# A thresholded attention with a two-layer MLP behind it: the first six periods and the order of the score products are rebuilt

## The chip, the cores and the metric

The kernel runs on one core of a Trainium2 chip. The core has a matrix engine (TensorE, PE in the profile, its weight loads PEld), VectorE (DVE), ScalarE (ACT), GpSimd (POOL), and a synchronisation engine (SyncE, SP) that issues most of the transfers. Each engine takes its own instructions strictly in the order in which the program gives them; engines wait for one another by semaphores. The metric is the device time of one execution in microseconds (us).

## What is computed

Eight batches of eight heads, 576 positions, head dimension 64. Scores are scaled products of q and k; each row keeps only the scores within tau = 0.02 of its maximum, and a softmax over what is left weighs v. The heads are put side by side, 4608 tokens of 512 numbers, and go through two matrix products with a leaky rectifier between them.

```python
scores = scale * np.matmul(q, k.transpose(0, 1, 3, 2))
thresh = np.max(scores, axis=-1, keepdims=True) - tau
scores = np.where(scores >= thresh, scores, -1000000000.0)
scores = scores - np.max(scores, axis=-1, keepdims=True)
attn = np.exp(scores)
attn = attn / (np.sum(attn, axis=-1, keepdims=True) + 1e-09)
x = np.matmul(attn, v)          # heads side by side: [4608, 512]
h = x @ w_in                    # [512, 2048]
out = np.maximum(0.01 * h, h) @ w_out
```

## The kernel before

**Splitting and turning.** q and k arrive as fp32 with positions on the partitions. A *unit* is one pair of heads of q or of k in one batch, or the 64-position tail of all pairs ("t"); a batch has ten units. Each is multiplied by 64 and split into a high fp16 part and a low one, so that three fp16 products (high-high, low-high, high-low) stand for one exact product. On GpSimd the split is `split_scale`, `split_high`, `split_low` (L144, L150, L154); `split_now` (L164, L165) does it on ScalarE and VectorE. TensorE then transposes the two parts into a PSUM tile `tp` (L183), and a copy, usually ScalarE's (L186, L190), puts them into `qT` or `kT`. The k tail is copied once more on GpSimd (L188).

**Periods.** 72 periods, nine for a batch: two blocks of 256 queries for each of the four head pairs, and one period for the tails. In a period the score products (L227, 24 of them, three for each of eight pieces) fill one PSUM tile `sc` of five banks: four places of 576 columns, two query halves c by two heads h. The two heads sit in the two row halves of TensorE. Two pieces of different heads share a bank; a signal, an empty GpSimd instruction (L246), keeps the later one behind the earlier. VectorE copies each place to SBUF and takes its minimum on the way (`copies`, L257; the sign is turned), makes the thresholds `th` (L259), and for three of the four places multiplies the exps by the mask (`weights`, L282). ScalarE makes the exps (L271), and for the fourth place the masked exps by itself (`exp_steep`, L276 and L277). The reciprocal of the sums (`rec`, L288) is spread over a strip of the weights by GpSimd (`widen`, L292), and one transposing DMA on SyncE (`turn_w`, L297) makes `wT`.

**Two periods later** PV multiplies v by `wT` (L309) and VectorE evacuates the product, scaled by the reciprocals (L321, L329), into a token group. Groups are queued for layer 1 (L349, with the leaky rectifier on ScalarE, L351) and layer 2 (L362, evacuated at L368): at most two calls of layer 1 and four of layer 2 in each period, and what is left over runs behind the last period. `tp`, `pv` and `hp` (layer 1's products) share two PSUM buffers, which go round in the order of the program.

**The order of the work** is written out by hand. The main loop gives each period's instructions; four tables (`loads_at`, `turns_at`, `pool_at`, `low_at`) say which loads, transposes and splits go into which period. In one period the loop gives, in this order: scores, the four copies, the widening and transposing DMA of the period before, low splits, loads, stores, transposes with their copies, GpSimd's other work, the exps with layers 1 and 2 between them, PV, the weights with the evacuation between the second and third, the reciprocal. Ahead of the loop the first loads are issued (pair 0 and 1 on SyncE's and ScalarE's queues, the k tail on SyncE's, the four parts of `w_in` on GpSimd's, right at the start), and the units pair 0 k, pair 0 q and k tail are split and turned:

```python
first = units(0)
for key in first[:3]:
    split_now(key)
turn(first[0])
turn(first[1], nc.vector.tensor_copy)
turn(first[2])
```

In what follows, the functions that the change touches are given with the line numbers of the profile.

## Time and profile before

| what | us |
|---|---|
| median of 3 runs (lowest, highest) | 527.41 (526.46, 530.69) |
| profiled execution: own time, span of its instructions | 526.85, 525.1 |
| busy: PE, VectorE, ScalarE, GpSimd | 472.8, 435.1, 422.3, 256.3 |
| first score copy (L257) starts | 16.04 |
| first layer-1 product (L349); last attention period's first copy | 63.78; 483.3 |
| scores of one period: 24 products at 26.0, at 83.5 | 3.10, 1.64 |
| transposing DMA, median from issue to landing | 5.9 |

The span runs from the first instruction to the last. Busy time is the time in which an engine executes; the time in which it waits is listed with the instruction that ended the wait. For this kernel the first 90 us differ from the rest: after them the periods nearly repeat every nine. A line of the timeline gives the start, the duration, the engine, the line, the operation, the tiles written and read, the number of instructions merged into the line, and in brackets the idle time before it and who ended it. SPq stands for SyncE's queue, where the duration is that of issuing.

### The profile page before, as it was taken

What the parts mean: (1) busy time and instruction counts of PE and PEld (TensorE: products, weight loads), DVE (VectorE), ACT (ScalarE), POOL (GpSimd) and SP (SyncE); (2) the same over time, 40 slices, a digit from 0 to 9 for tenths busy, and PEclk for the clock granted to TensorE, in tenths of its full rate; (3) what the DMA queues carried; (4) which work ended last, traced back from release to release, by engine and by line L of the source; (5) the groups of instructions that cost most, each with busy time, mean ns of one, the idle gap of its engine ahead of it and who ended that gap; (6) DMA issues with size and microseconds to landing.
All of it is one profiled execution on the core that took longest, in us unless ns stands there. A gap on an engine that the chain in (4) does not pass through costs nothing. (4 is left out here: it accounts for less than half of the span.)

```text
span 525.1 us, 18850 instructions
## 1 busy us (share of the span) xinstructions
PE 472.8 (90%) x7744; PEld 372.1 (71%) x7744; DVE 435.1 (83%) x1231; ACT 422.3 (80%) x714; POOL 256.3 (49%) x410
## 2 busy tenths in 40 slices
PE   4666768998989999999999999999999999999995
...
DVE  1778868999899999999899989999899989999300
...
GB/s 204 241 178 175 201 199 209 112 171 195 205 179 183 123 225 227 173 146 203 215 171 176 170 207 215 160 130 225 201 155 202 158 192 144 122 102 151 133 42 61
DMA packets 230806, 90.34 MB, mean 172 GB/s; under 512 B 201024, under 2 KB 227648, under 8 KB 230720
## 3 DMA queue, kind: packets, MB, share of 16 engines
...
## 5 line engine op out<-in xcount | busy, mean ns | idle before, releaser
L257 DVE TENSOR_SCALAR_CACHE_REDUCE s<-sc 128x576 f32<-128x576 f32 x288 | 199.0, 748 | 12.0 <-PE sc L227 11.5
L282 DVE SCALAR_TENSOR_TENSOR w<-s,th,e 128x576 f16<-128x576 f32 x216 | 184.2, 876 | 8.6 <-ACT e L271 1.1
L271 ACT ACTIVATE e<-s,mn 128x576 f16<-128x576 f32 x216 | 158.7, 773 | 20.2 <-DVE s L257 19.2
L362 PE MATMUL o<-wout,g 128*64 128x512 f16 x1152 | 148.9, 380 | 5.0 <-ACT osb L368 3.5
L349 PEld LDWEIGHTS <-win 128*64 128x64 f16 x2560 | 127.4, 110 | 29.2 <-issue 16.0
L349 PE MATMUL hp<-x,win 128*64 128x256 f16 x2048 | 134.4, 273 | 8.4 <-ACT kT L190 4.5
L227 PE MATMUL sc<-kT,qT 64*128 64x256 f16 (+7 forms) x1920 | 128.4, 298 | 12.0 <-DVE s L257 4.7
L292 POOL CAST w<-rec 128x256 f16<-128x256 f32 x72 | 28.7, 399 | 211.8 <-DVE rec L288 199.6
L227 PEld LDWEIGHTS <-qT 64*128 64x128 f16 (+1 forms) x1920 | 97.9, 101 | 35.0 <-issue 19.5
L351 ACT ACTIVATE g<-hp 128x512 f16<-128x512 f32 x144 | 84.6, 588 | 13.0 <-PE hp L349 13.0
L362 PEld LDWEIGHTS <-g 128*64 128x64 f16 x1152 | 69.6, 110 | 35.5 <-issue 8.5
L154 POOL TENSOR_TENSOR half<-scaled,half 128x512 f16<-128x512 f32 (+1 forms) x77 | 82.5, 1079 | 0.6
L309 PE MATMUL pv<-wT,v 128*64 128x256 f16 (+1 forms) x960 | 55.6, 251 | 12.2 <-DMA wT<-w 6.7
L309 PEld LDWEIGHTS <-v 128*64 128x64 f16 x960 | 44.6, 112 | 25.9 <-POOL v L105 5.3
L277 ACT ACTIVATE w<-s,minus_tau 128x576 f16<-128x576 f32 x72 | 55.8, 775 | 5.8
L276 ACT ACTIVATE s<-s,th 128x576 f32<-128x576 f32 x72 | 55.8, 775 | 0.9 <-DVE th L259 0.9
L183 PE MATMUL tp<-ident,half 128*64 128x128 f16 x1152 | 49.3, 236 | 8.0 <-ACT half L164 5.1
L150 POOL CAST half<-scaled 128x512 f16<-128x512 f32 (+1 forms) x77 | 52.1, 676 | 4.9
L183 PEld LDWEIGHTS <-half 128*64 128x64 f16 x1152 | 38.6, 119 | 22.1 <-issue 15.9
L190 ACT COPY kT<-tp 128x1024 f16<-128x1024 f16 x32 | 32.3, 1010 | 21.4 <-PE tp L183 21.4
L144 POOL TENSOR_SCALAR scaled<-raw 128x512 f32<-128x512 f32 x62 | 40.7, 657 | 10.2 <-DMA raw<-in_q_dram 8.3
L190 ACT COPY qT<-tp 128x1024 f16<-128x1024 f16 x31 | 31.4, 1014 | 14.1 <-PE tp L183 14.0
...
## 6 DMA issues: line engine op xcount, KB each, us to landing
...
win<-in_moe_w_in_dram POOLq DMA_DIRECT2D x4, 512.0 KB, 11.5
...
wT<-w SPq DMA_TRANSPOSE x72, 5.9
...
```

The source lines that it names most:

```text
L154: nc.gpsimd.tensor_tensor(out=halves[key][:, 1, 0:n, :, :], in0=scaled.pop(key)[:, 0:n, :, :], in1=halves[key][:, 0, 0:n, :, :], op=AX.sub ...
L183: nc.tensor.transpose(o, half[:, x, t, h, :], ident[:, :])
L190: copy(out=dst[:, :, p, ds(c0, 512)], in_=tp[:, :, :, :].rearrange("d x t p -> d x (t p)"))
L227: yield nc.tensor.matmul(out=o, lhsT=lhs, rhs=turned[st.b, "k"][rows, kx, pair, ds(key0, n)], start=(i == 0), stop=(i == 2), skip_group_ch ...
L257: nc.vector.tensor_scalar(out=st.s[t][:, :], in0=sc[:, ds(PLACE[t], 576)], scalar1=-1.0 / UNIT, scalar2=None, op0=AX.mult, op1=AX.min, acc ...
L271: nc.scalar.activation(out=st.e[t][:, :], in_=st.s[t][:, :], func=AF.Exp, bias=st.mn[:, n : n + 1], scale=-1.0)
L276: nc.scalar.activation(out=z, in_=z, func=AF.Prelu, bias=st.th[:, n : n + 1], scale=-1.0, alpha=1e20)
L282: nc.vector.scalar_tensor_tensor(out=w_of(st, t), in0=st.s[t][:, :], scalar=st.th[:, n : n + 1], in1=st.e[t][:, :], op0=AX.is_le, op1=AX.mult,
L309: nc.tensor.matmul(out=o, lhsT=v16[st.b % 2][:, 2 * c + u if st.tail else st.p, blk, :], rhs=rhs, start=(i == 0), stop=(i == 4), skip_grou ...
L349: nc.tensor.matmul(out=hp[ds(64 * c, 64), jj, :], lhsT=w_in16[:, i, ds(128 * j + 64 * c, 64)], rhs=g.x[:, i, :], start=(i == 0), stop=(i = ...
L351: nc.scalar.activation(out=g.g[:, ds(nj * u, nj), :], in_=hp[:, :, :], func=AF.Prelu, bias=0.0, scale=1.0, alpha=0.01)
L362: nc.tensor.matmul(out=g.o[ds(64 * c, 64), :], lhsT=g.g[:, j, ds(128 * m + 64 * c, 64)], rhs=w_out16[:, j, :], start=(j == 0), stop=(j == ...
```

## The change

The order and the place of work change; the amount of arithmetic doesn't.

- **Start.** The k tail is loaded first, on GpSimd's queue. The units are split, turned and copied one after another: k tail, pair 0 k, pair 0 q; the tail's and q's copies are VectorE's, k's is ScalarE's. Pair 1 is split by ScalarE and VectorE (`split_now`) where GpSimd did it; GpSimd splits pair 2 ahead of the loop and pair 3 in period 0, each one period sooner than before. `w_in`'s four loads move from the start into periods 1 and 2, `w_out`'s from periods 3 to 6 into 4 to 7. The v casts move one period ahead, the tail's first. The q tail's split and turn move from periods 2 and 3 to 6 and 7.
- **Batch 1's units** are turned in periods 3, 4, 5, 6, 6, 7, 8, 8, 9, 10 instead of two in each of 4 to 8; their scale and high part come two periods before, the low part one. Two of its loads come a period later.
- **Scores.** The order of the pieces changes, and the signal between the pieces that share a bank comes early, after the three products of a piece of place (1,1) instead of (1,0); in periods 0 to 3 it is an empty instruction of ScalarE. The first copy (place (0,0)) is given as soon as its own two pieces and the next one are out, and later products are declared free of it.
- **Every period.** The reciprocal of a period moves behind the second copy of the next one. The low splits come ahead of the widening. `turn` only transposes; `take` copies. Both transposes of a period are given first, then one copy, the first exp, the other copy.
- **Periods 2 to 5.** PV and its evacuation come ahead of layers 1 and 2 and of the weights, and a finished group is ready in the same period.

```diff
-    def load_tails(b, which):
+    def load_tails(b, which, eng=None):
         t = sb.tile([128, 2, 2, 64], FP32, tag="rawt", bufs=2, name="rawt")
         src = SRC[which][b, :, MAIN:S, :].rearrange("(u sh) p d -> u p sh d", u=2)
         for u in range(2):
-            nc.sync.dma_start(out=t[ds(64 * u, 64), :, :, :].rearrange("p s h d -> p (s h) d"), in_=src[u])
+            (eng or nc.sync).dma_start(out=t[ds(64 * u, 64), :, :, :].rearrange("p s h d -> p (s h) d"), in_=src[u])
...
-    def turn(key, copy=None):
-        copy = copy or nc.scalar.copy
+    def turn(key):
         b, p, which = key
-        dst, half = turned_of(b, which), halves.pop(key)
+        half = halves.pop(key)
         n = 2 if p == "t" else 4
-        c0 = 0 if which == "q" else 64
         if p == "t":
-            c0 = MAIN if which == "q" else 0
             tp = ps.tile([128, 2, 2, 2, 64], FP16, tag="h", bufs=2, name="tp")
         else:
             tp = ps.tile([128, 2, 4, 128], FP16, tag="h", bufs=2, name="tp")
...
                 for h in range(2):
                     o = tp[ds(64 * h, 64), x, :, t, :] if p == "t" else tp[ds(64 * h, 64), x, t, :]
                     nc.tensor.transpose(o, half[:, x, t, h, :], ident[:, :])
+        tps[key] = tp
+
+    def take(key, copy=None):
+        copy = copy or nc.scalar.copy
+        b, p, which = key
+        dst, tp = turned_of(b, which), tps.pop(key)
         if p == "t":
+            c0 = MAIN if which == "q" else 0
             for x in range(2):
                 copy(out=dst[:, x, :, ds(c0, 64)], in_=tp[:, x, :, :, :].rearrange("d u s p -> d (u s) p"))
             if which == "k":
                 nc.gpsimd.tensor_copy(out=dst[:, :, :, 576:640], in_=dst[:, :, :, 0:64])
         else:
+            c0 = 0 if which == "q" else 64
             copy(out=dst[:, :, p, ds(c0, 512)], in_=tp[:, :, :, :].rearrange("d x t p -> d x (t p)"))
...
+    TILES = ((0, 0), (0, 1), (1, 0), (1, 1))
+
     def scores(st):
 
+        st.mn = sb.tile([128, 4], FP32, tag="mn", bufs=2, name="mn")
+        st.th = sb.tile([128, 4], FP32, tag="th", bufs=2, name="th")
+        st.s, st.e = {}, {}
         (a00, a01), (b01, b00) = pieces(0, 0), pieces(0, 1)
         (a11, a12), (b12, b11) = pieces(1, 0), pieces(1, 1)
-        todo = [[(1, a12), (0, a00), (0, a01), (1, a11)], [(0, b00), (0, b01), (1, b11), (1, b12)]]
+        todo = [[(0, a00), (0, a01), (1, a11), (1, a12)], [(1, b12), (1, b11), (0, b01), (0, b00)]]
         todo = [[(c, x, i) for c, x in row for i in range(3)] for row in todo]
-        at_, signal = [0, 0], None
+        at_, signal, first = [0, 0], None, None
         while todo[0] or todo[1]:
             h = 1 if not todo[0] or (todo[1] and at_[1] < at_[0]) else 0
             c, x, i = todo[h].pop(0)
             at_[h] += x[1]
             for mm in product(st, c, h, x, i):
-                if (h, x) == (1, b12) and i == 0:
+                if first is not None:
+                    tc.declare_no_dep(mm.ins, first.ins, reason="other banks")
+                if (h, x) == (0, a12) and i == 0:
                     tc.add_manual_dep(mm.ins, signal.ins.name, BEHIND, reason="the row halves share a bank")
                 last = mm
-            if (h, x) == (0, a12) and i == 2:
-                signal = nc.gpsimd.nop()
+            if (h, x) == (1, b12) and i == 2:
+                signal = (nc.scalar if st.n < 4 else nc.gpsimd).nop()
                 tc.add_manual_dep(signal.ins, last.ins.name, BEHIND, reason="the row halves share a bank")
-
-    TILES = ((0, 1), (0, 0), (1, 0), (1, 1))
-
-    def copies(st):
-        st.mn = sb.tile([128, 4], FP32, tag="mn", bufs=2, name="mn")
-        st.th = sb.tile([128, 4], FP32, tag="th", bufs=2, name="th")
-        st.s = {}
-        for n, t in enumerate(TILES):
-            st.s[t] = sb.tile([128, 576], FP32, tag=f"s{n}", bufs=1, name="s")
-            nc.vector.tensor_scalar(out=st.s[t][:, :], in0=sc[:, ds(PLACE[t], 576)], scalar1=-1.0 / UNIT, scalar2=None,
-                                    op0=AX.mult, op1=AX.min, accum_out=st.mn[:, n : n + 1])
+            if (h, x) == (0, a11) and i == 2:
+                first = copy_min(st, 0)
+
+    def copy_min(st, n):
+        st.s[TILES[n]] = sb.tile([128, 576], FP32, tag=f"s{n}", bufs=1, name="s")
+        return nc.vector.tensor_scalar(
+            out=st.s[TILES[n]][:, :], in0=sc[:, ds(PLACE[TILES[n]], 576)], scalar1=-1.0 / UNIT, scalar2=None,
+            op0=AX.mult, op1=AX.min, accum_out=st.mn[:, n : n + 1])
+
+    def copies(st, before):
+        copy_min(st, 1)
+        if before:
+            recip(before)
+        copy_min(st, 2)
+        copy_min(st, 3)
         nc.vector.tensor_scalar(out=st.th[:, :], in0=st.mn[:, :], scalar1=1.0, scalar2=tau_f, op0=AX.mult, op1=AX.add)
         st.w = sb.tile([128, 2, 10, 128], FP16, tag="w", bufs=3, name="w")
         st.sum = sb.tile([128, 2, 2], FP32, tag="sum", bufs=3, name="sum")
-        st.e = {}
...
-    def finish(st):
+    def recip(st):
...
-    def evacuate(st, n):
+    def evacuate(st, ready):
...
-            l1q.extend((xg, u, nu, n + 1) for u in range(nu))
+            l1q.extend((xg, u, nu, ready) for u in range(nu))
...
     def split_at(n, key):
-        if key[0]:
-            at(pool_at, n - 2, lambda key=key: split_scale(key))
-            at(pool_at, n - 2, lambda key=key: split_high(key))
-            at(low_at, n - 1, lambda key=key: split_low(key))
-        else:
-            at(pool_at, n - 1, lambda key=key: split_pool(key))
-        at(turns_at, n, lambda key=key: turn(key))
+        at(pool_at, n - 2, lambda key=key: split_scale(key))
+        at(pool_at, n - 2, lambda key=key: split_high(key))
+        at(low_at, n - 1, lambda key=key: split_low(key))
+        at(turns_at, n, key)
 
     for b in range(1, B):
         base = PERB * (b - 1)
         for i, (s, w_) in enumerate(((0, "k"), (0, "q"), (1, "k"), (1, "q"))):
-            at(loads_at, base + ((-2, -1, 2, 3)[i] if b > 1 else (1, 1, 3, 3)[i]),
+            at(loads_at, base + ((-2, -1, 2, 3)[i] if b > 1 else (1, 1, 3, 4)[i]),
                lambda b=b, s=s, w_=w_: load_main(b, s, w_))
         for i, w_ in enumerate("kq"):
-            at(loads_at, base + ((-1, 5)[i] if b > 1 else (2, 4)[i]), lambda b=b, w_=w_: load_tails(b, w_))
+            at(loads_at, base + ((-1, 5)[i] if b > 1 else (2, 5)[i]), lambda b=b, w_=w_: load_tails(b, w_))
         for i, key in enumerate(units(b)):
-            split_at(base + 2 + 8 * i // 10 if b > 1 else base + 4 + i // 2, key)
+            split_at(base + 2 + 8 * i // 10 if b > 1 else (3, 4, 5, 6, 6, 7, 8, 8, 9, 10)[i], key)
     for b in range(B):
         base = PERB * (b - 1)
         if b:
             for s in range(2):
                 at(loads_at, base + 5 + s, lambda b=b, s=s: load_v(b, s))
             at(loads_at, base + 6, lambda b=b: load_vtails(b))
-        for p in range(NP):
-            at(pool_at, base + 8 + p if b else 2 + p // 2, lambda b=b, p=p: cast_v(b, p))
-        at(pool_at, base + 8 if b else 2, lambda b=b: cast_vtails(b))
-
-
+            for p in range(NP):
+                at(pool_at, base + 8 + p, lambda b=b, p=p: cast_v(b, p))
+            at(pool_at, base + 8, lambda b=b: cast_vtails(b))
+
+
+    load_tails(0, "k", nc.gpsimd)
     masks.make_identity(nc, ident[:, :])
     nc.gpsimd.memset(minus_tau[:, :], -tau_f)
     load_pair(0, "k", nc.sync)
     load_pair(0, "q", nc.scalar)
-    load_tails(0, "k")
+    load_pair(1, "k", nc.sync)
     load_pair(1, "q", nc.scalar)
-    load_pair(1, "k", nc.sync)
     for p in (2, 3):
         load_pair(p, "k", nc.sync)
         load_pair(p, "q", nc.sync)
...
     for t in v16:
         nc.gpsimd.memset(t[64:128, :, 4, :], 0.0)
         nc.gpsimd.memset(t[0:64, :, 5, :], 0.0)
+
+    first = units(0)
+    for key in (first[2], first[0], first[1]):
+        split_now(key)
+        turn(key)
+        take(key, None if key == first[0] else nc.vector.tensor_copy)
+    for key in first[3:5]:
+        split_now(key)
+    for key in first[5:7]:
+        split_pool(key)
+    for i, key in enumerate(first[3:9]):
+        at(turns_at, i // 2, key)
+    for key in first[7:9]:
+        at(pool_at, 0, lambda key=key: split_pool(key))
+    at(pool_at, 6, lambda: split_pool(first[9]))
+    at(turns_at, 7, first[9])
     for i in range(4):
-        load_w(i)
-        at(pool_at, 3 + i, lambda i=i: load_w(4 + i))
-
-    first = units(0)
-    for key in first[:3]:
-        split_now(key)
-    turn(first[0])
-    turn(first[1], nc.vector.tensor_copy)
-    turn(first[2])
-    for i, key in enumerate(first[3:]):
-        if i < 2:
-            split_pool(key)
-            at(turns_at, 0, lambda key=key: turn(key))
-        else:
-            split_at((0, 0, 1, 1, 2, 2, 3)[i], key)
+        at(pool_at, 1 + i // 2, lambda i=i: load_w(i))
+        at(pool_at, 4 + i, lambda i=i: load_w(4 + i))
+    at(pool_at, 1, lambda: cast_vtails(0))
+    for p in range(NP):
+        at(pool_at, 1 + p // 2, lambda p=p: cast_v(0, p))
+
+    def pv_of(n, ready):
+        if n >= PV_LAG and n - PV_LAG < N:
+            pv(periods[n - PV_LAG])
+            return lambda: evacuate(periods[n - PV_LAG], ready)
+        return lambda: None
 
     N = len(periods)
     n = 0
     while n < N + PV_LAG or l1q or l2q or stores:
         st = periods[n] if n < N else None
+        before = periods[n - 1] if 1 <= n <= N else None
+        early = n < 6
         if st:
             scores(st)
-            copies(st)
-        if 1 <= n <= N:
-            widen(periods[n - 1])
-            turn_w(periods[n - 1])
+            copies(st, before)
+        elif before:
+            recip(before)
         for f in low_at.get(n, []):
             f()
+        if before:
+            widen(before)
+            turn_w(before)
         for f in loads_at.get(n, []):
             f()
         while stores:
             store()
-        for f in turns_at.get(n, []):
-            f()
+        keys = turns_at.get(n, [])
+        for key in keys:
+            turn(key)
+        for key in keys[:1]:
+            take(key)
+        if st:
+            exp_plain(st, 0)
+        for key in keys[1:]:
+            take(key)
         for f in pool_at.get(n, []):
             f()
-        if st:
-            exp_plain(st, 0)
+        if early:
+            pv_of(n, n)()
         for half in range(2):
             if l1q and l1q[0][3] <= n:
                 layer1()
...
                     exp_plain(st, 2)
                 else:
                     exp_steep(st, 3)
-        if n >= PV_LAG and n - PV_LAG < N:
-            pv(periods[n - PV_LAG])
+        x = (lambda: None) if early else pv_of(n, n + 1)
         if st:
             weights(st, 0)
             weights(st, 1)
-        if n >= PV_LAG and n - PV_LAG < N:
-            evacuate(periods[n - PV_LAG], n)
+        x()
         if st:
             weights(st, 2)
-            finish(st)
         n += 1
```

2 lines of the change are left out of this document (1 added, 1 removed).

## The prediction

> **What bounds it now.** I read the page's busy shares first, then its 40 slices.
>
> ```profile
> PE 472.8 (90%) x7744; PEld 372.1 (71%) x7744; DVE 435.1 (83%) x1231; ACT 422.3 (80%) x714; POOL 256.3 (49%) x410
> ...
> PE   4666768998989999999999999999999999999995
> DVE  1778868999899999999899989999899989999300
> ```
>
> The slices are 13 us long. PE is full from the eighth on and has holes only before. The windows view puts a number on the middle:
>
> ```profile
> 86.40:435.00 348.60, 335.02 (x5735) 265.77 (x5732) 323.33 (x919) 311.35 (x526) 188.30 (x300) 1.00 0.87 180
> ```
>
> From period 9 to 62 PE (first pair of numbers) idles 13.6 us in 349, VectorE (third) 25. PE executes in order and its work is fixed, so the end moves only by PE idle time that goes or comes. It idles 33 us before 100 us (5.1 ahead of its first instruction, the rest gaps), 13.5 between 100 and 480. The waits up to 100 us name the holes (total, times, longest):
>
> ```profile
> DVE s L257 <- PE sc L227: 11.5, 4, 7.8
> PE pv L309 <- DMA wT<-w: 6.2, 2, 3.4
> PE pv L309 <- POOL v L105: 4.8, 2, 4.3
> PE sc L227 <- POOLq L246: 3.5, 3, 2.3
> ```
>
> I mark time by c(n), the first score copy (L257) of period n on the timeline: 16.0, 23.0, 30.6, 41.1, 47.7, 54.3, 61.9, 69.4, 79.4, 86.4 for n = 0 to 9. The 54 periods from there to 435.1 last 6.46 on average, so periods 2 (10.5) and 7 (10.0) are the bad ones. The lines behind them:
>
> ```profile
> 15.18 0.82 PE L227 MATMUL sc<-kT,qT 64*128 64x256 f16 x5 [2.31 <-POOLq L246]
> ...
> 16.04 0.76 DVE L257 TENSOR_SCALAR_CACHE_REDUCE s<-sc 128x576 f32<-128x576 f32 x1 [7.81 <-PE sc L227]
> ...
> 24.03 3.14 SPq L297 DMA_TRANSPOSE wT<-w  x1
> ...
> 27.22 0.57 SPq L72 DMA_DIRECT2D raw<-in_k_dram  x1
> ...
> 31.51 0.62 POOL L144 TENSOR_SCALAR scaled<-raw 128x512 f32<-128x512 f32 x1 [0.35 <-DMA raw<-in_k_dram]
> ...
> 34.30 2.49 POOL L105 CAST v<-vraw 128x256 f16<-128x256 f32 x4
> ...
> 62.65 8.74 SPq L297 DMA_TRANSPOSE wT<-w  x1
> ...
> 75.51 0.83 PE L309 MATMUL pv<-wT,v 128*64 128x256 f16 x10 [3.36 <-DMA wT<-w]
> ```
>
> The first copy waits for all 24 products, and these for a signal queued on POOL behind splits. In period 2 POOL waits for batch 1's k, which SP could issue only behind the transpose of period 0; the v casts come after that and PV of period 0 ends at 38.1. In period 7 a transpose shares the DMA with weight loads and lands 12.8 after its issue.
>
> **The start.** k tails go first, on POOL's queue. No row has them there. Bounds: 2.5 from issue to landing (SP's quickest tail load, at 34.99) and 8.2 (POOL's first weight load, at 2.70). I take 5.0 as the landing time, near SP's load, because the tails are small and nothing is ahead of them. The Trainium skill, page "DMA: Bandwidth & Descriptors", section "Anatomy of one DMA — SWDGE (gpsimd) path", gives about 2.0 us plus size. By that estimate the tails are there before pair 0's k (4.6) and all of the start is 0.4 earlier. No row here shows it alone.
> Then the tail, k and q go one after another, where before they overlapped. ScalarE: tail 5.0-5.5, k 5.6-6.2 (0.33 a piece). VectorE: tail and its copies to 6.7, k to 7.4. PE turns k by 8.0; ScalarE copies it (0.99) to 9.1 and only then splits q, to 9.8; VectorE to 10.2, PE 10.9, copy (0.68) 11.65. Scores start at 11.75, against 10.38 before: 1.4 lost. Behind that signal stand the period's transposed copies and exps, which need PE's transposes, and those come after the products anyway; so it holds up nothing. The two tail issues delay POOL's identity by 1.2 to 1.7 (its weight issues took 0.6 to 0.84), hidden until the first transpose at 5.6. Cold, 19 products take 2.5 and 24 take 3.1 (rows at 10.38 and 25.98). The signal now follows the split of pair 1 on ScalarE, done by 11.1, so the 2.3 stall goes; the first copy waits for 19 of 24. c(0) = 14.3, 1.8 earlier, with 13.3 to 16 as ends.
>
> **Periods 0 and 1.** PE turns pair 1 behind the scores, to 16.8. ScalarE: k copy, one exp, q copy, two exps, steep pair, to 21.9. Its signal for period 1 is queued behind all that, so the last products run 21.9 to 22.5; c(1) = 21.5, and the second copy waits for 22.5. The reciprocal now stands behind that copy: 23.3. It was 22.7. Widening 23.6, transpose issued 24.0: as before. c(2) comes out at 29.1 the same way (row 30.6).
>
> **POOL in periods 1 to 3 is the step that decides.** Its list for period 1 begins with the split of batch 1's k, whose load is still issued on SP behind that transpose: 24.0 + 3.1, landing 4.2 later (row at 27.22), 31.4. Behind the waiting instruction are queued two weight loads, the v tail casts, the casts of pairs 0 and 1, the low split, and then the widening of period 1, which was ahead of this wait before. By rows: scale and high 1.3, two loads 1.2, tails 0.85, pair 0 1.25: 36.2, PV of period 0 ends 36.9 (was 38.1). In the first six periods its evacuation stands ahead of the weights on VectorE, so these follow at 37.4 and end about 40.2: c(3) = 40.3, 0.8 gained. Pair 1 1.25, low 1.15: widening 38.6, transpose 39.1. It was 31.2. It lands 7.4 later (4.9 unloaded, 12.8 the longest; the nearest beside a weight load was 9.2 and 7.0, and four weight loads now fall in 33 to 50): 46.5. PV of period 1 can't run before, PE and VectorE stand, then 0.9 + 0.4 + three weights at 0.8: c(4) = 50.3, 2.6 late, from 48 to 53. Period 2 in the same way (widening 45.6, landing 53.5): c(5) = 57.2, 2.9 late. From period 3 POOL's list is short and the wait is gone; two layer-1 units now run in period 5. c(6) +2.5, c(7) +1.6. In period 7 the 3.4 wait can recur, since the w_out loads come a period later, beside v: I take half, so c(8) and c(9) come out even with before. **Early: 0, ends -4 and +5.**
> The weight loads are issued in busy periods: four in the quiet start took 2.37, 0.59 each, and w_out beside work 0.82 to 0.84, so 1.0 more, in the ends. The Trainium skill speaks against it: "SBUF — State Buffer", section "SBUF: two separate sides", says that POOL cannot write descriptors while VectorE holds the port pair they share. By that each issue would wait out a VectorE instruction (0.75 to 1.15), 3 to 4.6 for the four, and c(5) would be that much later still; the 0.82 rows say a quarter of it.
>
> **Periods 9 to 13.** Layer 1 of the first token group moves from periods 6-9 to 5-8. The next group is ready at period 10 in both, so the end's backlog stays; period 9 loses two units and 12 to 13 four layer-2 calls. PE would save 3.5, but VectorE alone needs about 5.8 a period: 0.8 gained.
>
> **The steady periods.**
>
> ```profile
> DVE rec L288 <- ACT w L277: 10.7, 23, 0.9
> ...
> PE hp L349 <- ACT kT L190: 6.2, 10, 0.7
> ...
> PE o L362 <- ACT osb L368: 2.8, 8, 0.6
> ...
> PE pv L309 <- DMA wT<-w: 0.5, 1, 0.5
> ```
>
> The reciprocal no longer waits for ScalarE's sum ahead of the first copy; VectorE gains 0.2 to 0.5 a period. PE gains only what it idled for VectorE's sake: the osb waits, unnamed gaps ahead of layer 2 (1.5), waits for evacuations and copies (2.4). That is 6.7; I take 4.5. The 6.2 of hp waits stay, as PE waits there for the first transposed copy in both. In exchange the reciprocal is 1.5 later, and so are widening, transpose and landing. PV starts about 3.45 after c and has waited once; late by 1.5, the transposes of periods 14, 15, 33, 51, 59 and 60 (latencies with queueing of 8 to 9.3) make it wait 0.1 to 1.5 each: 3.0 lost. The second transposed copy behind the first exp frees its PSUM buffer about when layer 1 needs it (0.68 + 0.9 against 1.75): 0.5 lost. **Steady: -1.0.** With nothing new it would be -4.5, with no gain +3.5.
>
> **Sum.** 526.85 (span 525.1 and 1.7 around it) + 0 - 0.8 - 1.0 = 525.0. The median 527.41 is 0.6 above that execution, inside its runs' 526.46 to 530.69, so I keep 525.
>
> **Rivals.** *POOL's order costs nothing that wasn't lost anyway* (27%): the start's 1.8 stays, period 7's 3.4 does not return, the 0.8 and the steady 4.5 come without new waits: 526.85 - 10.5 = 516.4. For it: the weight loads leave the start, and PE idles 28 in gaps before 100. Against: widening of period 1 behind the load, by program order.
> *Transposes late* (23%): one mechanism, PV waiting for wT. It decides once a transpose takes over 7.8 from issue to landing (with the 1.5, that reaches PV's start). Rows beside loads: 9.2, 12.8, 8.1. If the one of period 1 takes 10 the early loss is 5 and period 7 gives none back; steady +3: 526.85 + 8 = 535.
> *The freed first copy still waits for all products*: 0.6 less at the start, steady gain 2 less: about 527.6, inside the forecast's case (50%, 522 to 530).
>
> **Numbers.** A measurement tells about 1% (5.3 us) from no change. Faster by more 0.30 (the first rival and the low edge of the forecast), within 0.47, slower 0.23. Range 517 to 534.
>
> **What would show it.** Right: first copy near 14.3; POOL idle at the first split of batch 1 until about 31; period 1's transpose issued near 39 and PV waiting for wT or VectorE for PV around 46; c(5) later than 54.3, c(9) near 86; no wait of rec for ScalarE; a few PV waits for wT later. Wrong: c(5) below 53, or c(9) beyond 89, or the steady period below 6.3 or above 6.55.

## The result, and the profile after

The changed kernel takes **546.75 us** (median of 4, 545.83 to 550.07) against 526.93 (median of 4, 525.85 to 530.69) for the kernel before on the same chip: 1.037 times as long, 95% interval 1.031 to 1.044. The forecast was 525.0 with a range of 517 to 534. The profiled execution spans 544.0 against 525.1.

The page's busy shares and the 40 slices (now 13.6 us each) answer the first fence of the prediction:

```profile
PE 473.3 (87%) x7744; PEld 367.3 (68%) x7744; DVE 454.0 (83%) x1237; ACT 423.3 (78%) x716; POOL 270.7 (50%) x406
...
PE   1645586897999999998999989998999999999995
DVE  1865978899999998999989999999899999999300
```

PE is as busy as before (473.3 against 472.8), so all of the loss is idle PE. VectorE and POOL are busier by 18.9 and 14.4 us with almost the same instructions; that is a first hint that some of them became slower.

The time is split by c(n), the start of the first score copy of period n (L265 in the changed kernel, L257 before), as in the prediction.

| stretch, us | before | after | difference |
|---|---|---|---|
| start to c(0) | 16.04 | 20.77 | +4.7 |
| c(0) to c(5) | 38.2 | 45.2 | +7.0 |
| c(5) to c(9) | 32.1 | 31.5 | -0.6 |
| c(9) to c(63), the steady periods | 348.7 | 357.4 | +8.7 |
| c(63) to c(71), periods that turn nothing | 48.3 | 46.1 | -2.2 |
| c(71) to the end | 41.7 | 43.1 | +1.4 |

**The start.** The timeline of the changed kernel up to the first copy (start and duration in us, engine, line, operation; the bracket is the wait before it and what ended it):

```profile
1.26 1.47 POOL L86 DMA_DIRECT2D rawt<-in_k_dram  x2 [0.82 <-POOLq L552]
...
8.81 1.28 ACT L164 ACT_TABLE_LOAD   x1 [8.81 <-DMA rawt<-in_k_dram]
...
10.11 0.51 ACT L164 ACTIVATE half<-rawt 128x128 f16<-128x128 f32 x2
...
18.06 2.79 DVE L165 SCALAR_TENSOR_TENSOR half<-raw,half 128x256 f16<-128x256 f32 x4
18.20 3.06 PE L232 MATMUL sc<-kT,qT 64*128 64x384 f16 x24 [0.79 <-DVE qT L195]
...
20.77 0.74 DVE L265 TENSOR_SCALAR_CACHE_REDUCE s<-sc 128x576 f32<-128x576 f32 x1
```

In the kernel before, ScalarE's queue began like this:

```profile
1.80 1.28 ACT L164 ACT_TABLE_LOAD   x1 [1.80 <-issue]
...
4.61 1.34 ACT L164 ACTIVATE half<-raw 128x256 f16<-128x256 f32 x4 [1.52 <-DMA raw<-in_k_dram]
```

Two things put the first split at 10.11, where the prediction had 5.0. The two tail loads, issued at 1.26 and 2.08 on POOL's queue, land at 7.58 and 8.74. Only then does ScalarE's table load run. Before, the first activation waited for one load, and the table load ran at 1.80, ahead of that wait. Now the first activation needs two loads; the trace has the wait for the second of them as an instruction of its own (8.76), and the table load comes behind it. From the first split on, everything is in series. The freed first copy starts at 20.77, half a microsecond before the last product ends at 21.26. The products it needs end at 20.61; VectorE is splitting pair 1 until 20.85 (the row at 18.06), with no idle time before the copy.

**Periods 1 to 8.** The same view from 28 to 60 us:

```profile
37.46 0.62 POOL L144 TENSOR_SCALAR scaled<-raw 128x512 f32<-128x512 f32 x1 [7.56 <-DMA raw<-in_k_dram]
...
41.24 1.62 PE L324 MATMUL pv<-wT,v 128*64 128x256 f16 x10 [5.35 <-POOL v L105]
...
43.71 4.04 SPq L312 DMA_TRANSPOSE wT<-w  x1
...
49.84 7.23 SPq L312 DMA_TRANSPOSE wT<-w  x1
...
52.49 1.28 PE L324 MATMUL pv<-wT,v 128*64 128x256 f16 x10 [6.08 <-DMA wT<-w]
...
57.07 0.40 POOL L144 TENSOR_SCALAR scaled<-rawt 128x256 f32<-128x256 f32 x1 [7.26 <-DMA rawt<-in_k_dram]
...
57.59 0.50 PE L232 MATMUL sc<-kT,qT 64*128 64x256 f16 x5 [1.49 <-POOLq L258]
```

This is the chain that the prediction called the step that decides: POOL waits 7.56 for batch 1's k, the v casts come late and PV of period 0 waits 5.35 for them, the widening and so the transpose of period 1 are late, and PV of period 1 waits 6.08 for its landing. Two things were not in the prediction: the transpose of period 2, where SP needs 7.23 to issue it (3.1 unloaded), and POOL's second long wait, for k tails, which holds up POOL's signal of period 4. The waits of the whole stretch up to 110 us (total, times, longest):

```profile
PE pv L324 <- DMA wT<-w: 9.4, 4, 6.1
PE pv L324 <- POOL v L105: 5.3, 1, 5.3
PE pv L324 <- DVE s L265: 4.6, 1, 4.6
PE sc L232 <- ACT qT L195: 4.5, 2, 2.2
PE sc L232 <- POOLq L258: 3.1, 3, 1.5
DVE s L265 <- PE sc L232: 2.1, 4, 1.0
```

The first copies' wait for products fell from 11.5 to 2.1 (7.81 of the 11.5 was the very first copy, ahead of which VectorE is now busy with pair 1). PE's waits at PV rose: 19.3 for `wT`, v and VectorE, where the rows of before have 6.2 for `wT` and 4.8 for v.

**The steady periods.** The windows view between c(9) and c(63), in the columns of the prediction's second fence (PE, PEld, VectorE, ScalarE, POOL):

```profile
97.45:454.82 357.37, 336.32 (x5732) 263.44 (x5728) 336.38 (x918) 311.64 (x526) 208.25 (x301) 1.00 0.87 178
```

With one instruction less, VectorE is busy for 336.4 us instead of 323.3; POOL for 208.3 instead of 188.3 with one more. The granted clock is 1.00 in both stretches, so the clock is not what differs. The page's groups say where (busy us, mean ns of one). Before:

```profile
L282 DVE SCALAR_TENSOR_TENSOR w<-s,th,e 128x576 f16<-128x576 f32 x216 | 184.2, 876 | 8.6 <-ACT e L271 1.1
L154 POOL TENSOR_TENSOR half<-scaled,half 128x512 f16<-128x512 f32 (+1 forms) x77 | 82.5, 1079 | 0.6
```

After:

```profile
L297 DVE SCALAR_TENSOR_TENSOR w<-s,th,e 128x576 f16<-128x576 f32 x216 | 197.9, 937 | 11.7 <-ACT e L286 4.0
L154 POOL TENSOR_TENSOR half<-scaled,half 128x512 f16<-128x512 f32 (+1 forms) x75 | 93.8, 1259 | 63.2 <-PE sc L232 62.6
```

VectorE's weights (w = e where s passes the threshold) and POOL's low halves (half = scaled minus high half) have both become slower on average, and the low halves now wait 62.6 us in all for score products. The change moved them ahead of the widening on POOL, behind POOL's signal, which waits for products of PE. The timeline shows what that does. Before, a low half runs under the score copies (around 279.6 us):

```profile
279.11 0.73 DVE L257 TENSOR_SCALAR_CACHE_REDUCE s<-sc 128x576 f32<-128x576 f32 x1
279.63 1.16 POOL L154 TENSOR_TENSOR half<-scaled,half 128x512 f16<-128x512 f32 x1
...
283.14 0.81 DVE L282 SCALAR_TENSOR_TENSOR w<-s,th,e 128x576 f16<-128x576 f32 x1
```

After, it runs under the weights of the period before. Around 301.6 us, in a period that takes 6.97 where its counterpart takes 6.15, the low half starts first and keeps its 1.16, while the weights take twice their time:

```profile
300.61 0.81 DVE L297 SCALAR_TENSOR_TENSOR w<-s,th,e 128x576 f16<-128x576 f32 x1
...
301.51 1.16 POOL L154 TENSOR_TENSOR half<-scaled,half 128x512 f16<-128x512 f32 x1 [1.45 <-PE sc L232]
301.68 1.60 DVE L297 SCALAR_TENSOR_TENSOR w<-s,th,e 128x576 f16<-128x576 f32 x1
```

Six microseconds earlier the weights start first. They keep their 0.81, and the low half is the longer one:

```profile
295.32 0.81 DVE L297 SCALAR_TENSOR_TENSOR w<-s,th,e 128x576 f16<-128x576 f32 x1
295.57 1.58 POOL L154 TENSOR_TENSOR half<-scaled,half 128x512 f16<-128x512 f32 x1 [1.92 <-PE sc L232]
```

So it goes through the steady periods of the changed kernel: weights that start under a running low half take 1.36 to 1.71 (16 of them), and low halves that start under running weights take 1.58 in the median (28 of the 48 of this size), 1.16 without an overlap.

Added up over periods 18 to 62, low halves and weights overlap for 0.0 us before and 25.9 after. The Trainium skill, page "SBUF — State Buffer", section "Who interferes with whom", says that a VectorE instruction with two SBUF inputs contends with a GpSimd (POOL) instruction that reads SBUF, for a port pair that one of them holds at a time. The trace agrees: whichever starts first keeps its time (1.16 and 0.81 above), and the other is longer (1.60 and 1.58).

The predicted wait of the steady periods came and is larger: PV's waits for `wT` add up to 4.5 us between 97 and 480 (0.5 before; 3.0 more was predicted). The reciprocal no longer waits for ScalarE (10.7 before, no such row now).

### The profile page after: what moved, and what is told of

The parts are those of the page before. It is cut to its first block, busy times and chain, and to the rows that moved or that the text cites. A ratio compares the mean times of both kernels' runs of the same rounds, so it can differ in the third digit from the quotient of the medians.

```text
span 544.0 us, 18997 instructions
## 1 busy us (share of the span) xinstructions
PE 473.3 (87%) x7744; PEld 367.3 (68%) x7744; DVE 454.0 (83%) x1237; ACT 423.3 (78%) x716; POOL 270.7 (50%) x406
## 5 line engine op out<-in xcount | busy, mean ns | idle before, releaser
L265 DVE TENSOR_SCALAR_CACHE_REDUCE s<-sc 128x576 f32<-128x576 f32 x288 | 204.2, 744 | 5.2 <-PE sc L232 2.5
L297 DVE SCALAR_TENSOR_TENSOR w<-s,th,e 128x576 f16<-128x576 f32 x216 | 197.9, 937 | 11.7 <-ACT e L286 4.0
L364 PEld LDWEIGHTS <-win 128*64 128x64 f16 x2560 | 129.1, 111 | 32.9 <-issue 19.9
L364 PE MATMUL hp<-x,win 128*64 128x256 f16 x2048 | 136.2, 275 | 11.6 <-ACT kT L195 9.1
L232 PE MATMUL sc<-kT,qT 64*128 64x384 f16 (+7 forms) x1920 | 128.2, 295 | 11.0 <-ACT qT L195 4.5
L154 POOL TENSOR_TENSOR half<-scaled,half 128x512 f16<-128x512 f32 (+1 forms) x75 | 93.8, 1259 | 63.2 <-PE sc L232 62.6
L232 PEld LDWEIGHTS <-qT 64*128 64x128 f16 (+1 forms) x1920 | 94.7, 100 | 37.3 <-issue 14.5
L180 PE MATMUL tp<-ident,half 128*64 128x128 f16 x1152 | 48.3, 229 | 13.9 <-ACT half L164 11.9
L195 ACT COPY kT<-tp 128x1024 f16<-128x1024 f16 x32 | 32.3, 1010 | 31.6 <-PE tp L180 31.4
L180 PEld LDWEIGHTS <-half 128*64 128x64 f16 x1152 | 36.8, 114 | 29.1 <-issue 13.4
L344 DVE TENSOR_TENSOR x<-pv,wT 128x256 f16<-128x256 f32 x64 | 26.9, 420 | 23.8 <-PE pv L324 23.7
```

What stands on the lines that cost most here:

```text
L154: nc.gpsimd.tensor_tensor(out=halves[key][:, 1, 0:n, :, :], in0=scaled.pop(key)[:, 0:n, :, :], in1=halves[key][:, 0, 0:n, :, :], op=AX.sub ...
L180: nc.tensor.transpose(o, half[:, x, t, h, :], ident[:, :])
L232: yield nc.tensor.matmul(out=o, lhsT=lhs, rhs=turned[st.b, "k"][rows, kx, pair, ds(key0, n)], start=(i == 0), stop=(i == 2), skip_group_ch ...
L265: return nc.vector.tensor_scalar(out=st.s[TILES[n]][:, :], in0=sc[:, ds(PLACE[TILES[n]], 576)], scalar1=-1.0 / UNIT, scalar2=None, op0=AX. ...
L297: nc.vector.scalar_tensor_tensor(out=w_of(st, t), in0=st.s[t][:, :], scalar=st.th[:, n : n + 1], in1=st.e[t][:, :], op0=AX.is_le, op1=AX.mult,
L364: nc.tensor.matmul(out=hp[ds(64 * c, 64), jj, :], lhsT=w_in16[:, i, ds(128 * j + 64 * c, 64)], rhs=g.x[:, i, :], start=(i == 0), stop=(i = ...
```

## The experiments

The theories. **Low halves**: the steady 8.7 come from POOL's low halves beside VectorE's weights, and nothing else of the new order costs there. Its rival is the new order itself (late reciprocal, second transposed copy behind an exp). **Start**: tails, table load and the serial order delay everything behind them; its rival is that PE has slack there, so that what is gained at c(0) is lost again by c(9). **POOL's order**: the early loss is batch 1's split ahead of the widening; its rival is that it comes from transposes beside weight loads, wherever POOL's order puts them.

All runs in one table; the kernels are told below. The ratio is against the kernel before, run on the same chip beside it; most kernels ran only twice, so their intervals are wide, and c(n) and the span are of the one profiled execution.

| run | c(0) | c(9) | c(63)-c(9) | c(71)-c(63) | span | ratio, interval |
|---|---|---|---|---|---|---|
| before | 16.04 | 86.40 | 348.7 | 48.3 | 525.1 | |
| after | 20.77 | 97.45 | 357.4 | 46.1 | 544.0 | 1.037 (1.031 to 1.044) |
| e1 after, low halves held | 20.66 | 105.79 | 349.7 | 46.1 | 544.8 | 1.045 (1.031 to 1.058) |
| e2 before, low halves first | 15.67 | 86.28 | 354.6 | 48.3 | 530.9 | 1.016 (1.007 to 1.025) |
| e3 after, old start | 13.25 | 95.24 | 357.5 | 46.1 | 541.9 | 1.035 (1.027 to 1.043) |
| e4 after, old batch 1 | 20.32 | 98.90 | 355.5 | 46.1 | 543.8 | 1.041 (1.031 to 1.051) |
| e5 after, w_in at the start | 21.54 | 98.31 | 355.6 | 46.1 | 543.1 | 1.041 (1.034 to 1.049) |
| e6 after, e3+e4+e5 | 13.58 | 91.33 | 355.9 | 46.1 | 536.3 | 1.023 (1.015 to 1.031) |
| e7 e6 + held | 13.00 | 89.71 | 349.3 | 46.1 | 528.1 | 1.013 (1.005 to 1.022) |
| e8 e6, old reciprocal and low halves | 13.24 | 92.81 | 352.6 | 48.3 | 535.4 | 1.023 (1.017 to 1.029) |
| e9 after, all weights at the start | 21.22 | 90.99 | 355.9 | 46.1 | 536.2 | 1.024 (1.020 to 1.028) |
| e10 before, all weights at the start | 16.14 | 90.38 | 349.6 | 48.2 | 529.9 | 1.013 (1.008 to 1.017) |
| e11 before, late reciprocal, low halves first and held | 16.16 | 85.28 | 355.2 | 46.5 | 529.9 | 1.015 (1.005 to 1.025) |
| e12 before, freed copy | 11.91 | 83.97 | 349.5 | 48.3 | 523.5 | 1.004 (1.002 to 1.006) |
| e13 after, e3+e9+held | 13.24 | 89.61 | 348.5 | 46.1 | 527.2 | 1.007 (1.004 to 1.010) |
| e14 e13, weights a little later | 11.71 | 92.13 | 348.8 | 46.1 | 530.0 | 1.011 (1.004 to 1.018) |
| e15 after, tails on SP's queue | 18.05 | 95.14 | 355.8 | 46.1 | 540.0 | 1.029 (1.018 to 1.039) |
| e16 after, table load early | 19.56 | 96.76 | 356.1 | 46.1 | 542.1 | 1.030 (1.019 to 1.040) |
| e17 e12 + late reciprocal at the end | 12.18 | 85.25 | 349.2 | 45.7 | 523.1 | 0.997 (0.993 to 1.000) |
| e18 e17, w_out in period 2 | 12.38 | 86.98 | 349.4 | 45.7 | 525.1 | 0.998 (0.995 to 1.001) |

### The steady periods: e1, e2, e11, e8

**e1_low_hold**: the changed kernel, and the first low half of a period waits for the last weights of the period before.

```diff
-        nc.gpsimd.tensor_tensor(out=halves[key][:, 1, 0:n, :, :], in0=scaled.pop(key)[:, 0:n, :, :],
-                                in1=halves[key][:, 0, 0:n, :, :], op=AX.subtract)
+        low = nc.gpsimd.tensor_tensor(out=halves[key][:, 1, 0:n, :, :], in0=scaled.pop(key)[:, 0:n, :, :],
+                                      in1=halves[key][:, 0, 0:n, :, :], op=AX.subtract)
+        if hold:
+            tc.add_manual_dep(low.ins, hold.pop().ins.name, BEHIND, reason="behind the weights")
...
         if st:
-            weights(st, 2)
+            hold[:] = [weights(st, 2)]
```

> The changed kernel with one wait more: the first low split of a period (GpSimd, L154) waits for the last weights instruction of the period before, so that low splits run under the score copies and not under the weights. Theory 1 (low splits and weights slow each other): the mean of the weights falls from 937 ns to below 890, that of L154 from 1259 to about 1100, and the growth of the lag behind the kernel before from period 9 to 63, 8.7 us, falls below 4. Theory 2 (the later reciprocal makes wT late and PV wait): widening is as late as before or later, so the growth stays at 8 or more, though the weights get shorter.

The groups of e1 (its line numbers are four higher on VectorE and two on POOL):

```profile
L301 DVE SCALAR_TENSOR_TENSOR w<-s,th,e 128x576 f16<-128x576 f32 x216 | 184.2, 872 | 16.6 <-ACT e L290 8.8
L156 POOL TENSOR_TENSOR half<-scaled,half 128x512 f16<-128x512 f32 (+1 forms) x75 | 79.5, 1067 | 112.3 <-PE sc L236 64.2 <-DVE w L301 43.8 <-DMA out_dram<-osb 3.7
```

Both durations are back at those of before, their overlap in periods 18 to 62 is 0.0, and the steady stretch takes 349.7: 7.7 of the 8.7 are gone. PV's waits for `wT` in that stretch fall to 1.1 (4.5 in the changed kernel from period 9 to 62), so most of that growth also came with the low halves and not with the late reciprocal. The kernel as a whole is not faster, because periods 5 to 8 took 41.8 instead of 31.5. There the transposes of periods 4 to 6 needed 13.5, 17.4 and 17.3 from issue to landing (9.5, 7.1 and 10.1 in the changed kernel), and PV waited:

```profile
PE pv L328 <- DMA wT<-w: 19.3, 5, 6.5
```

The hold is the only edit, so this loss came with it: the transposes now fall otherwise among the loads of `w_out` and of batch 1. It is not a fixed price of the hold. In e7, below, the same edit leaves periods 5 to 8 at 33.4, against 34.5 without it.

**e2_before_low_first** is the other side: the kernel before with this one step of the change.

```diff
+        for f in low_at.get(n, []):
+            f()
         if 1 <= n <= N:
             widen(periods[n - 1])
             turn_w(periods[n - 1])
-        for f in low_at.get(n, []):
-            f()
```

> The kernel before with one thing of the change: the low splits ahead of the widening on GpSimd. The reciprocal stays where it was. Theory 1: the weights' mean rises from 876 to 910 or more, and the time rises by 4 to 9 us. Theory 2: the reciprocal is early, so it stays within 2 us.

The steady stretch grows by 5.9, to 354.6, with c(9) where it was:

```profile
L282 DVE SCALAR_TENSOR_TENSOR w<-s,th,e 128x576 f16<-128x576 f32 x216 | 195.2, 926 | 8.9 <-ACT e L271 1.6
L154 POOL TENSOR_TENSOR half<-scaled,half 128x512 f16<-128x512 f32 (+1 forms) x77 | 96.2, 1259 | 92.6 <-PE sc L227 85.5 <-DMA vrawt<-in_v_dram 6.4
```

The low halves take the same 1259 ns as in the changed kernel, and the weights are 50 ns longer, 216 times. Taken out of the changed kernel the overlap gives 7.7 back (6.6 from e6 to e7, below), put into the kernel before it costs 5.9: the low halves under the weights are the cause of most of the steady loss.

**e11_before_rec_hold**: the kernel before with the reciprocal in the next period, behind the second copy, and with low halves ahead of the widening but held.

```diff
+            if n == 1 and before:
+                finish(before)
...
-            finish(st)
+            hold[:] = [weights(st, 2)]
```

> The kernel before with the reciprocal behind the second copy of the next period, and the low splits ahead of the widening but behind the last weights of the period before; start, first periods, score order and copies as before. If the late reciprocal frees VectorE and the low splits under the copies cost nothing: 345 to 348 from period 9 to 63 (before 348.7), 46 to 47 from 63 to 71 (48.3), time 2 to 5 lower. Rival (PV waits for the later wT take back what VectorE gains): 349 or more, time the same or higher.

Without any overlap (weights 878, low halves 1080 ns) the steady stretch still takes 355.2, and the last periods 46.5 instead of 48.3. That is the rival's outcome. PE's waits from 85 to 480 us have `PE sc L231 <- POOLq L250: 4.4, 6, 1.9`, the score products waiting for POOL's signal, where e1 has 2.0, and 3.9 at PV for `wT`, where e1 has 1.1. So with held low halves the changed kernel is within 1.0 of before in these periods, and here, with the late reciprocal, 6.5 are lost without any overlap; which of the two kernels' differences makes that so was not taken apart.

**e8_early_old_recend** is e6 (below) with the reciprocal back at the end of the period and the low halves back behind the widening.

```diff
-        if before:
-            recip(before)
...
         if before:
             widen(before)
             turn_w(before)
+        for f in low_at.get(n, []):
+            f()
...
             weights(st, 2)
+            recip(st)
```

> As the run with the three early things as before, with the reciprocal at the end of its period and the low splits behind the widening, both as before; kept are the order of the score products, the first copy free of later ones, the split of transposes and copies, the early PV. By the prediction's steady term without the late reciprocal: PE waits less for osb and evacuations, 346 to 348 from period 9 to 63, time 522 to 526. Rival (PE is the limit and the freed copy buys nothing): 348 to 350, time within 2 of before.

The weights are at 878 ns, the last periods at 48.3 and the end at 41.7, as before. The late reciprocal therefore gives 2.2 in the periods that turn nothing and costs 1.4 behind them. The steady stretch takes 352.6, outside both expectations: better than with the overlap (355.9 in e6) and 3.3 worse than with the hold and the late reciprocal (349.3 in e7). What makes those 3.3 stays open.

### The start: e3, e15, e16, e12

**e3_start_old**: the changed kernel with the old order of the start (tails on SP's queue behind pair 0, three units side by side).

```diff
-    load_tails(0, "k", nc.gpsimd)
...
     load_pair(0, "q", nc.scalar)
+    load_tails(0, "k")
...
-    for key in (first[2], first[0], first[1]):
+    for key in first[:3]:
         split_now(key)
+    for key in first[:3]:
         turn(key)
-        take(key, None if key == first[0] else nc.vector.tensor_copy)
+        take(key, nc.vector.tensor_copy if key == first[1] else None)
```

> The changed kernel with the start as before: k tails on SyncE's queue, and pair 0 k, pair 0 q, k tail split first and turned after. Theory 1 (tail on GpSimd's queue, table load behind it, one unit after another): first score copy at 13 to 14 instead of 20.8, and the end 6 to 8 us earlier. Rival (the rest of the change refills the gap, because periods 1 to 5 wait for loads and transposes): the first copy is earlier but the end gains under 3.

c(0) is 7.5 earlier, so the new start itself costs 7.5 at the first copy. (It could have been more: the products that the first copy needs end at 11.74 here, and VectorE splits pair 1 until 13.33.) At c(9) only 2.2 of them are left, because c(9) - c(0) grew from 76.7 to 82.0. The transposes of periods 6 and 7 took 13.3 and 12.5 to land (10.1 and 9.7 in the changed kernel). The span gains 2.2, the rival's outcome.

**e15_tail_sp** moves the tail loads alone; **e16_table** takes the table load alone, by a copy of one column whose result nothing uses.

```diff
-    load_tails(0, "k", nc.gpsimd)
+    load_tails(0, "k")
```

> The changed kernel, its k tails still first in line and still computed first, but loaded over SyncE's queue. Theory (the landing on POOL's queue is the larger part of the late first copy): the tails land at about 6.5 instead of 8.74, the table load starts as early, and the first copy is about 2 earlier, near 18.7. Rival (the serial order of tail, pair and pair sets the first copy, whatever the landing): first copy within 0.5 of 20.8. The steady periods as in the changed kernel (c(63) - c(9) about 357).

```diff
+    idle = sb.tile([128, 1], FP32, name="idle")
+    nc.scalar.activation(out=idle[:, :], in_=minus_tau[:, :], func=AF.Copy, bias=0.0, scale=1.0)
```

> The changed kernel with one small ScalarE copy ahead of everything (of minus_tau, 128 x 1), which the result doesn't use, so that the table load doesn't stand behind the wait for the tail. Theory: the first take of the tail starts 1.28 earlier and the first copy with it, near 19.5. Rival: VectorE's part of the same take or its splits end last anyway, and the first copy moves by less than 0.4. The rest as in the changed kernel.

On SP's queue the tails are there at 6.08 and c(0) is 18.05, 2.7 earlier. With the table load out of the way c(0) is 19.56, 1.2 earlier. The timeline of e15:

```profile
6.08 1.28 ACT L164 ACT_TABLE_LOAD   x1 [6.08 <-DMA rawt<-in_k_dram]
...
7.38 0.51 ACT L164 ACTIVATE half<-rawt 128x128 f16<-128x128 f32 x2
...
9.13 1.16 DVE L165 SCALAR_TENSOR_TENSOR half<-raw,half 128x256 f16<-128x256 f32 x2
...
12.38 1.61 DVE L165 SCALAR_TENSOR_TENSOR half<-raw,half 128x256 f16<-128x256 f32 x2 [2.09 <-ACT half L164]
...
15.47 3.06 PE L232 MATMUL sc<-kT,qT 64*128 64x384 f16 x24 [0.78 <-DVE qT L195]
```

From the first split to the first product it takes 8.09 in e15 and in the changed kernel, so the landing and the table load only shift this chain. If the two add up, which was not run together, the 7.5 of e3 are 2.7 of queue, 1.2 of table load, and 3.6 that are left for the serial order.

**e12_before_free**: the kernel before with the new order of the products, the first copy freed of the later ones.

```diff
-        todo = [[(1, a12), (0, a00), (0, a01), (1, a11)], [(0, b00), (0, b01), (1, b11), (1, b12)]]
+        todo = [[(0, a00), (0, a01), (1, a11), (1, a12)], [(1, b12), (1, b11), (0, b01), (0, b00)]]
...
+                if first is not None:
+                    tc.declare_no_dep(mm.ins, first.ins, reason="other banks")
...
+            if (h, x) == (0, a11) and i == 2:
+                first = copy_min(st, 0)
```

> The kernel before with the new order of the score products and the first copy free of later ones, alone. Freed copy of use: c of period 0 earlier by 0.5 or more, 48.3 from period 63 to 71 falls to 46.5 to 47.5, time 1 to 4 lower. Rival (PE is the limit, or the new order shifts the signal): all within 1 of before.

c(0) is 11.91 instead of 16.04. At c(9) 2.4 are left, and the steady stretch doesn't gain (349.5 against 348.7). The last periods stay at 48.3, where 46.5 to 47.5 was expected. The profiled execution is 1.6 shorter in span, but the median of eight is 526.52 against 525.45 before (ratio 1.002 to 1.006): alone, the freed copy is no gain.

### The early periods: e4, e5, e9, e10, e14

**e4_batch1_old** puts the loads and splits of batch 1 and the last split of batch 0 back into their old periods.

```diff
...
-            split_at(base + 2 + 8 * i // 10 if b > 1 else (3, 4, 5, 6, 6, 7, 8, 8, 9, 10)[i], key)
+            split_at(base + 2 + 8 * i // 10 if b > 1 else base + 4 + i // 2, key)
...
-    at(pool_at, 6, lambda: split_pool(first[9]))
-    at(turns_at, 7, first[9])
+    at(pool_at, 2, lambda: split_pool(first[9]))
+    at(turns_at, 3, first[9])
```

> The changed kernel with the schedule of batch 1's splits, turns and loads, and of batch 0's q tail, as before, so that no split of batch 1 stands ahead of the v casts and of the widening of period 1. Theory 1 (GpSimd's wait for the load of batch 1): PV of period 0 no longer waits for v, the transpose of period 1 is issued within 3 us of its reciprocal, and the time from the first copy of period 0 to that of period 5 falls from 45.2 to 38 to 40. Rival (the four w_in loads in periods 1 and 2 slow the transposes): their latency stays at 8 to 9 us and those five periods stay at 43 or more.

c(5) - c(0) is 44.0 instead of 45.2 and c(9) is 98.90, later than in the changed kernel. POOL's wait ahead of the v casts is gone, as the theory says, and PV no longer waits for v. But POOL now issues the first two loads of w_in at 29.54, just ahead of the transpose of period 0:

```profile
29.54 1.18 POOL L114 DMA_DIRECT2D win<-in_moe_w_in_dram  x2
29.62 9.72 SPq L312 DMA_TRANSPOSE wT<-w  x1
...
42.34 1.27 PE L324 MATMUL pv<-wT,v 128*64 128x256 f16 x10 [6.31 <-DMA wT<-w]
```

That transpose lands after 12.6 instead of 5.1, and PV of period 0 waits for it, to 42.34 instead of 41.24. One delay was exchanged for another, so this run does not tell what the plan of the splits costs by itself.

**e5_w_start** issues the four loads of w_in at the start, as before; **e9_changed_all_w_start** all eight; **e10_before_all_w_start** does that in the kernel before.

```diff
+    for i in range(4):
+        load_w(i)
+
     first = units(0)
...
-        at(pool_at, 1 + i // 2, lambda i=i: load_w(i))
```

> The changed kernel with the four w_in loads back at the start, on GpSimd's queue behind its memsets; all else as changed. Theory 3 (the w_in loads in periods 1 and 2 slow the transposes and hold up GpSimd's casts): the latencies of the transposes of periods 1 to 3 fall from 8.6 to 9.4 to 5 to 6, and the time from the first copy of period 0 to that of period 5 from 45.2 to 40 or less. Rival (GpSimd's wait for batch 1's k and the late widening suffice): it stays at 43 or more, with short latencies.

```diff
+    for i in range(8):
+        load_w(i)
+
     first = units(0)
...
-    for i in range(4):
-        at(pool_at, 1 + i // 2, lambda i=i: load_w(i))
-        at(pool_at, 4 + i, lambda i=i: load_w(4 + i))
```

> The changed kernel with all eight weight loads (w_in and w_out) at the start, on GpSimd's queue. Theory 4 (transposes that share the DMA with weight loads take 7 to 14 us, and PV of two periods later waits for them): from period 3 on the latencies are 5 to 7, the first copy of period 9 comes 62 to 66 after that of period 0 (changed 76.7, before 70.4), though the start is later by the loads. Rival (the wait of GpSimd for batch 1's k and the late reciprocal are enough): 73 or more with short latencies.

In the kernel before, the same by `for i in range(8)` in place of 4:

> The kernel before with all eight weight loads at the start. Theory 4: the 3.4 wait of period 7 goes, no transpose of the first nine periods takes over 8 us, period 9 starts 2 to 4 earlier, the time is 2 to 4 lower. Rival (the loads at the start push q, k and v back): the first copies come later by as much, and the time stays within 2.

The times from issue to landing of the transposes of periods 0 to 8 tell these apart:

| run | 0 | 1 | 2 | 3 | 4 | 5 | 6 | 7 | 8 |
|---|---|---|---|---|---|---|---|---|---|
| before | 5.0 | 5.3 | 4.9 | 9.2 | 7.0 | 12.8 | 8.1 | 6.3 | 4.9 |
| after | 5.1 | 8.7 | 9.4 | 8.6 | 9.5 | 7.1 | 10.1 | 9.7 | 4.9 |
| e5 | 5.0 | 4.9 | 5.0 | 6.7 | 8.5 | 7.8 | 14.0 | 14.0 | 4.9 |
| e9 | 9.5 | 4.9 | 5.0 | 7.5 | 4.8 | 6.6 | 6.9 | 6.4 | 4.9 |
| e10 | 11.4 | 7.8 | 4.9 | 6.6 | 5.0 | 6.7 | 5.2 | 5.0 | 5.4 |

With w_in gone from periods 1 and 2, the transposes of periods 1 and 2 take 4.9 and 5.0, and c(5) - c(0) falls from 45.2 to 39.5. That is 5.7 gained, and periods 5 to 8, where w_out runs beside the transposes of periods 6 and 7 (14.0 each), take it away again. With w_out gone as well (e9), c(9) - c(0) is 69.8 instead of 76.7, 0.6 less than before the change, though not the 62 to 66 that were expected. So 6.9 us of the early loss go with the weight loads, with POOL's order as the change has it and at its late start. With the early start c(9) - c(0) is 82.0 in e3, and 76.4 with eight loads at the start and the hold (e13, below). In e10 periods 5 to 8 take 27.2 instead of 32.1, for the same reason, yet the kernel is slower, by more than the rival allowed. The transpose of period 0 holds SP for 9.34, batch 1's k is issued behind it, POOL waits 10.06 for that k with the v casts behind, and PV of period 0 waits 13.3:

```profile
PE pv L309 <- POOL v L105: 13.3, 1, 13.3
```

**e14_start_wmid_hold** is e13 (below) with w_in issued ahead of pair 2's splits and w_out in period 0.

```diff
-    for i in range(8):
+    for i in range(4):
         load_w(i)
...
+    for i in range(4):
+        at(pool_at, 0, lambda i=i: load_w(4 + i))
```

> As the run before, but the loads of w_in are issued by POOL just ahead of pair 2's splits and those of w_out in period 0, behind the loads of v. Theory (the loads cost where they run beside the transposes of periods 4 to 8, and only there): c(9) about 83, span about 522, time 522 to 526. Rival (what matters is that they are out of the way altogether; in the first periods they delay v and q): c(3) later than 45, c(9) at 88 or later, time 528 or more.

The earliest first copy of all (11.71) and still c(9) at 92.13: the transpose of period 0 now takes 13.8, SP issues batch 1's k behind it, and POOL waits 15.42 for that before it casts v. This is the rival's outcome.

### The parts together: e6, e7, e13, e17, e18

**e6_early_old** undoes start, plan of batch 1 and w_in together (the diffs of e3, e4 and e5); **e7_early_old_hold** holds the low halves too (e1's diff); **e13_start_allw_hold** is e3's start, e9's loads and e1's hold.

> The changed kernel with three things as before: the start (k tails on SyncE, three units side by side), the w_in loads at the start, the schedule of batch 1. The order in every period stays as changed, low splits ahead of the widening and the reciprocal late. If the early loss lies in those three: the first copy of period 9 comes at 84 to 88 (before 86.4, changed 97.5), the later part is as slow as in the changed kernel (357 from period 9 to 63, 349 before), the time 533 to 537. Rival (early PV, the late reciprocal and the signal on ScalarE cost the early time): period 9 at 92 or later.

> As the run with the three early things as before, and the low splits wait for the last weights of the period before. If the loss is these two parts and nothing else, it is gone: 349 to 350 from period 9 to 63, the weights below 890 ns, time 524 to 528. If the late reciprocal costs by itself, 352 or more and PV waits for wT.

> The changed kernel with three edits at once: the old order of the start (tails on SyncE's queue, three units side by side), all eight weight loads issued at the start, and the first low split held behind the last weights of the period before. Theory (the three losses are separate and add up): first copy 13.3, c(9) - c(0) about 70 so c(9) about 83, c(63) - c(9) 349.5, c(71) - c(63) 46.1, end 43.1 after it: span about 522, time 522 to 526, the time of before or a little under. Rival (they are not additive: loads at the start make raw or v late, as with all loads at the start before): c(9) at 88 or later, time 528 or more.

e6 takes off 7.7 us of span and e7 15.9 of the 18.9. Both missed their expectations in the early periods (c(9) is 91.33 in e6, not 84 to 88), and e7's time, a median of 531.42, is above the 524 to 528 expected. In e6 the transpose of period 1 takes 8.6 with w_in out of the way: batch 1's k and q, 512 KB each, were issued just ahead of it, so it isn't weight loads alone that slow a transpose. What is left in e7 is in the early periods: c(9) is 89.71 against 86.40, and the steady stretch, the last periods and the end add up to 438.4 against 438.7. e13 missed its expectation: c(9) is 89.61, not 83. Its steady part is the best of all (348.5), but the early gains don't add up:

```profile
PE pv L328 <- POOL v L105: 13.5, 1, 13.5
```

With an early start and eight loads ahead, SP takes 13.05 us to issue the v tails, batch 1's k lands late and POOL waits 11.15 for it with the v casts behind. Period 2 takes 21.0 us (10.5 before).

**e17_free_late** leaves out what lost: the kernel before with the freed copy (e12) and the late reciprocal in periods 63 to 71 only.

```diff
+        if before and before.n >= 63:
+            finish(before)
...
-            finish(st)
+            if n < 63:
+                finish(st)
```

> The kernel before with the new order of the products (first copy freed of later ones), and with the reciprocal moved into the next period for periods 63 to 71 only. Theory (the two gains stand by themselves): c(9) near 84, c(63) - c(9) 349.5, c(71) - c(63) 46.1, end 43.1 after it: span 522.7, time 524 to 526, ratio 0.995 to 1.002. Rival (the late reciprocal gains only beside the changed order of PV): c(71) - c(63) stays at 48.3 and the ratio at 1.003 or above.

c(71) - c(63) is 45.7 and the rest behind it 43.0, so the late reciprocal gives 1.3 net without the other parts; c(9) is 1.2 earlier than before. The ratio is 0.9965, interval 0.9934 to 0.9995. That is the best kernel of this study; its gain is a third of a per cent, with an interval that all but reaches 1.

**e18_free_late_wout** moves w_out into period 2 of e17, behind the casts of v.

```diff
-        at(pool_at, 3 + i, lambda i=i: load_w(4 + i))
+        at(pool_at, 2, lambda i=i: load_w(4 + i))
```

> The run before with the four loads of w_out issued by POOL in period 2, behind the casts of v, instead of one in each of periods 3 to 6. Theory (transposes beside weight loads are what stretches periods 4 to 8): latencies of the transposes of periods 4 to 7 at 7 or less, c(9) near 81, span near 520, ratio 0.990 to 0.997. Rival (four loads at once delay the transposes of periods 2 and 3 and the raw loads of batch 1 by as much): c(9) 84 or later, ratio 0.997 or more.

The transposes of periods 4 to 7 land after 5.3, 6.7, 4.9 and 4.9, and periods 5 to 8 take 27.2, as the theory has it. The one of period 2 pays for them:

```profile
38.44 3.08 POOL L117 DMA_DIRECT2D wout<-in_moe_w_out_dram  x4
...
43.58 9.13 SPq L307 DMA_TRANSPOSE wT<-w  x1
...
56.05 1.28 PE L319 MATMUL pv<-wT,v 128*64 128x256 f16 x10 [5.66 <-DMA wT<-w]
```

c(9) is 86.98, later than in e17. In every place that was tried the loads cost about what they cost elsewhere.

## Why the prediction was wrong

In spans the forecast was 1.8 less and the result is 18.9 more. The 20.7 between are 6.5 at the start, 4.6 from c(0) to c(9), and 9.7 behind it. Two of the prediction's own signs of being wrong came: c(9) beyond 89 (97.45) and a steady period above 6.55 (6.62).

**The start** (c(0) = 14.3, measured 20.77). The direction of the chain was right, its entry wrong. *"I take 5.0 as the landing time"*: it was 8.8, so 3.8 late. From issue to landing the two took 6.3 and 6.7, inside the bounds of 2.5 to 8.2 (SP's quickest tail load in the trace took 2.3, not 2.5, which changes nothing); the end of 16 for c(0) did not carry the upper bound through. "Nothing is ahead of them" was no reason for the lower one, since the pairs' loads of 256 KB were issued at the same time on two other queues. The size estimate of the Trainium skill that the prediction put beside it, page "DMA: Bandwidth & Descriptors", section "Anatomy of one DMA — SWDGE (gpsimd) path", was farther off still. The **table load** (1.28) was no term of the sum at all; in the trace of before it runs at 1.80, ahead of any wait for a load. The last 1.35 is the chain from split to products, 8.09 instead of 6.75: VectorE's pair splits take 0.75 on average, where they took 0.42 before, and POOL's splits run beside them now. That this is the same contention as in the steady periods was not tried by itself. The first copy came 2.6 after the first product, as predicted, and partly by luck: VectorE's splits of pair 1, which the sum left out, happened to end as the 19 products did; in e3 they held the first copy for 1.5.

**Periods 0 to 8** (c(9) was put even with before, so 1.7 more from c(0) to c(9); measured 6.3 more). The named chain came, link by link: batch 1's split waits for its load, v and widening behind it, the transpose late, PV waiting for `wT`. c(5) - c(0) was put at 42.9 and is 45.2. Two terms failed. The transposes beside w_in were put at 7.4 and took 8.7 and 9.4. And *"c(8) and c(9) come out even with before"* failed: the stretch from c(5) to c(9) gave back 0.6, not the 2.9 that were booked, with three of the transposes of periods 4 to 7 at 9.5 to 10.1. That the weight loads beside the transposes carry this loss, at this start and in this order of POOL's, is shown by e5 and e9. What POOL's order of the splits costs by itself is not shown, since e4 brought a new collision. The rival *Transposes late* had the mechanism, with a point of decision at 7.8 (8.7 came), and nearly the size: c(9) 5 late with a start 1.7 early is 6.7 from c(0) to c(9), where 6.3 came. The Trainium skill, which the prediction set against its price of the loads, page "SBUF — State Buffer", section "SBUF: two separate sides", says that POOL cannot write descriptors while VectorE holds the port pair they share. As the prediction read it, each issue would have been longer by a VectorE instruction. The four w_in loads took 0.55 to 0.61 each to issue, two of them beside a running VectorE instruction and two beside an idle one, so no run shows it.

**Steady** (-1.0 together with the last periods, and -0.8 for periods 9 to 13; measured +7.9 from c(9) to the end, of which +2.8 in periods 9 to 13). The failed step is one that was not there: the move of the low halves ahead of the widening stands in the change and has no price in the sum. It costs 6 to 8 (e2, e1). Without the overlap periods 9 to 13 are at 31.7 in e1 and 31.6 in e7, against 31.5 before, so the 0.8 did not come either. The terms that did stand were small and partly right. The reciprocal's wait for ScalarE is gone; its gain came only in the last periods (2.2, less 1.4 at the end). PV's waits for `wT` were put at 3.0 and grew by 4.0, and without the overlap by about 1 (1.1 in e1, 1.7 in e7). The gain of 4.5 in the steady periods did not come: without the overlap e1 and e7 take 349.7 and 349.3, against 348.7 before.

**The first rival**, *POOL's order costs nothing that wasn't lost anyway*, fell with the 7.56 and 6.08 waits. *The freed first copy still waits for all products* fell too: it started at 20.77 with the last product ending at 21.26. No forecast or rival reached 546, because all of them had the steady periods within 5 us of before.

PV ahead of the MLP work and the early signal on ScalarE had no run of their own. The signal waits of the first periods are small (0.2 in all on ScalarE's queue, 3.1 on POOL's), and more can't be said of them.
